# Moving small VectorE passes to GpSimd and ScalarE, and transposing all keys of the first batch by TensorE, in a fused agent-attention and mixture-of-experts kernel

## The chip, the cores and the metric

The kernel runs on one core of one Trainium2 chip. The metric is the time of one execution in device microseconds. A core has TensorE (PE in the profile, its weight loads PEld), VectorE (DVE), ScalarE (ACT), GpSimd (POOL) and SyncE (SP), which here only issues transfers. Each engine works through its own queue in order and waits at semaphores for the others.

## The reference

For each of B = 4 batches of N = 11456 tokens with C = 128 channels there are 49 agents. The agents attend to the keys, and the queries attend to the agents; the result is the input `x` of a mixture of 8 experts of width 1024, where each token goes to the one expert with the highest logit.

```python
def _attn_ref(q, k, v, agents):
    scale = 1.0 / np.sqrt(q.shape[-1])
    def sm(a, b):
        s = scale * (a @ b.transpose(0, 2, 1))
        s = s - s.max(-1, keepdims=True)
        e = np.exp(s)
        return e / (e.sum(-1, keepdims=True) + 1e-09)
    return sm(q, agents) @ (sm(agents, k) @ v)

# x: the attention's result, 45824 x 128
xn = x / (norm(x) + 1e-06); en = expert_emb / (norm(expert_emb) + 1e-06)
logits = xn @ en.T / tau
expert_idx = argmax(logits)
gate_w = exp(logits - max)[expert_idx] / (sum(exp(logits - max)) + 1e-09)
out[i] = gate_w[i] * (relu(x[i] @ w1[e]) @ w2[e])      # e = expert_idx[i]
```

## The kernel before

**Tiling.** A batch is cut into 12 units, eleven of 8 x 128 tokens and one of 2 x 96. A unit of keys, queries or values is loaded as one tile (`kt`, `qt`, `vt`; L114). The FFN goes by tiles of 4 x 128 tokens, 23 a batch, in 8 steps of 128 hidden columns each: 184 steps a batch, 736 in all.

**Precision.** The fp32 operands of the large products are split into two float16 parts, a high part and the remainder. A unit of keys or queries goes through `split`: ScalarE squares it for its size (L297), four small VectorE passes on one column (`half_scale`, L179 to L186) make a power of two `hsc` and its inverse `hiv`, ScalarE writes the scaled high part (L301), GpSimd multiplies and subtracts for the low part (L303, L304), and SP issues a DMA transpose (L309). Then TensorE has three float16 products for each 128 tokens (`scores`, L318 to L320). For queries, the inverse scale is multiplied with `escale` (L186), which holds the attention's scale. In a second way, `k1_f32`, TensorE transposes the fp32 unit itself (`pe_T`, L364), VectorE and ScalarE copy the result from PSUM, and TensorE scores it in fp32 (L382).

**Stages.** Nothing of the FFN can start until batch 0 has its agent values, since they are folded into the expert's weights. So there is a prelude: the 12 key units' scores (`k1`), the maximum over keys (`k_max`: a reduce, a transpose by TensorE, L151, L154, and the copy `pm`, L156), the 12 value units (`k2_unit`: `kd` = exp of the scores less the maximum, L400 and L402, and `avp`, `avx`, L408 to L414), then `av_chain` and `pick_expert`, which choose the batch's main expert, load its weights (`w1s`, `w2s`) and split them into `gh`, `gl`, `w2h`, `w2l`. Of batch 0's keys, units 1, 3, 5 and 7 (`K16`) go by `split` with `quick`, where VectorE makes the low part and ScalarE's own queue issues the DMA transpose; the other eight go by `k1_f32`. Between the value units stand other units, in a table `BETWEEN`: two queries of batch 0 and five key units of batch 1.

**Steady state.** In an FFN step TensorE makes `hp` (L722, L723), ScalarE `hh` = relu (L726), VectorE `hl`, the low part (L727), and four steps later (LAG) TensorE adds `yp` (L744 to L746) into one of two PSUM accumulators. After 8 steps `ffn_out` multiplies `yp` by the tokens' gates `gs` on VectorE (L759) and stores it. Beside the steps run the other queries (`queries`) and the keys and values of the next batch (`keys`), each a generator that issues a few instructions at a time. A query unit's softmax over agents (L572 to L576) gives `e`, which is split in two (L580 VectorE cast, L581 GpSimd), transposed (`tt`) and multiplied for the routing (`rtp`, `rtg`, `rt`, L598 to L617). For each group of one or two units `route_group` (L621) makes the gates `gs`: it takes norm, logits, their maximum and the softmax in small passes of 2 to 16 columns, or 8 times as many for the logits. There are 7 groups a batch. `mark_strays` and `stray` treat the tokens whose expert is not the main one.

**Order.** The order on each engine is set when the program is built: a scheduler with a simulated timeline places what the generators issue; in the prelude SP's order is that of the code.

## Time and profile before

| | |
|---|---|
| time, median of 3 executions | 1150.92 us (1150.88 to 1152.09) |
| time of the profiled execution | 1146.91 us, its span 1145.1 us |
| busy in the span: TensorE / VectorE / ScalarE / GpSimd | 1031.5 / 866.8 / 712.7 / 515.4 us |
| HBM traffic | 75.80 MB read, 23.53 MB written |

The table says how long each engine worked, not which one set the time; that is read stage by stage, from the rows in which an engine waits and what released it. In rows of the trace a start in us stands first, then the duration, the engine, the line, the operation and the tiles (out<-in), and in brackets the idle time ahead of it with what ended it. The profiled execution is 4.0 us shorter than the median of the others.

### The profile page before, as it was taken

The page shows a single profiled execution, that of the slowest core. Times are in us where ns is not written, and L with a number is a line of the kernel's source. Part 1 is how long each engine was busy: PE and PEld are TensorE (multiplying, and loading weights), DVE is VectorE, ACT ScalarE, POOL GpSimd, SP SyncE. Part 2 cuts the span into 40 slices and gives each one's busy share as a digit, 9 for nine tenths or more (in the row PEclk, how much of TensorE's full clock was granted, in tenths as well). Part 3 has the DMA queues.
Part 4 walks back from the last instruction along what each step waited for, and adds up shares of the span by engine and source line. Part 5 has one row for each costly group of instructions (what it writes and reads, how often), then busy time and mean ns, then how long its engine had stood idle before and what let it go on. Part 6 is the DMA issues. An engine that isn't in the chain of part 4 may idle for free.

```text
span 1145.1 us, 34081 instructions
## 1 busy us (share of the span) xinstructions
PE 1031.5 (90%) x13878; PEld 815.1 (71%) x13878; DVE 866.8 (76%) x2056; ACT 712.7 (62%) x1338; POOL 515.4 (45%) x449
## 2 busy tenths in 40 slices
PE   4677788999998888889999889999999799999997
PEld 4666566777777766667777667777778577887776
DVE  5446787877787778768688688877678889787785
ACT  4454967776657866756654876665455756655553
POOL 2262688756512986535430677354221624242100
PEclk9557899999999899999999899999999899999999
DMA  9959879953456997654433997733203534331100
GB/s 322 181 150 166 266 163 235 240 141 104 80 105 221 206 230 139 147 103 119 92 87 80 271 240 176 150 72 80 59 22 108 119 65 137 100 81 46 41 29 33
DMA packets 292264, 154.72 MB, mean 135 GB/s; under 512 B 216635, under 2 KB 268939, under 8 KB 292107
## 3 DMA queue, kind: packets, MB, share of 16 engines
q1 hardware_dynamic: 283723, 150.44, 54.9%
q10 hardware_dynamic: 8320, 2.10, 1.3%
q8 instruction: 109, 1.79, 0.6%
q14 instruction: 48, 0.39, 0.1%
q0 software_dynamic: 64, 0.00, 0.0%
HBM read 75.80 MB, written 23.53 MB: 87 GB/s over the span
## 4 chain that ended last, share of the span: by engine, by line
PE 53%; DMA 14%; issue 11%; DVE 9%; POOL 7%; ACT 4%; SPq 1%; ACTq 0%; POOLq 0%; DVEq 0%
PE hp L722 9%; PE yp L744 9%; PE yp L746 9%; PE yp L745 9%; PE hp L723 9%; PE avp L408 4%; DMA tt<-e 4%; DMA kt<-in_k_dram 3%; DVE hl L727 3%; DMA kT<-ks 2%; DMA qT<-qs 2%; POOL qt L303 2%; POOL kt L303 1%; POOL ks L304 1%; ACT hh L726 1%
## 5 line engine op out<-in xcount | busy, mean ns | idle before, releaser
L727 DVE SCALAR_TENSOR_TENSOR hl<-hp,hh 128x512 f16<-128x512 f32 (+1 forms) x736 | 479.6, 669 | 112.3 <-ACT hh L726 91.9
L726 ACT ACTIVATE hh<-hp 128x512 f16<-128x512 f32 (+1 forms) x736 | 416.5, 585 | 223.7 <-PE yp L745 132.4
L744 PE MATMUL yp<-w2h,hh 128*128 128x128 f16 (+1 forms) x2880 | 523.3, 220 | 6.4 <-ACT hh L726 6.2
L745 PE MATMUL yp<-w2l,hh 128*128 128x128 f16 (+1 forms) x2880 | 523.0, 220 | 2.7 <-DVE w2l L533 2.7
L746 PE MATMUL yp<-w2h,hl 128*128 128x128 f16 (+1 forms) x2880 | 522.4, 220 | 0.0
L744 PEld LDWEIGHTS <-hh 128*128 128x128 f16 (+1 forms) x2880 | 285.2, 99 | 61.5 <-ACT hh L726 8.5
L746 PEld LDWEIGHTS <-hl 128*128 128x128 f16 (+1 forms) x2880 | 285.6, 99 | 46.5 <-issue 3.9
L722 PE MATMUL hp<-tt,gh 128*128 128x512 f16 (+1 forms) x736 | 279.2, 379 | 40.0 <-DVE hl L727 35.3
L745 PEld LDWEIGHTS <-hh 128*128 128x128 f16 (+1 forms) x2880 | 285.2, 99 | 38.4 <-issue 0.3
L723 PE MATMUL hp<-tt,gl 128*128 128x512 f16 (+1 forms) x736 | 278.8, 379 | 0.0
L615 POOL TENSOR_TENSOR rt<-rt,qe 128x392 f32<-128x392 f32 (+1 forms) x48 | 46.3, 965 | 163.2 <-ACT rt L614 163.1
L303 POOL TENSOR_TENSOR qt<-qt,hsc 128x1024 f32<-128x1024 f32 (+1 forms) x46 | 81.9, 1783 | 66.2 <-ACT qs L301 52.8
L723 PEld LDWEIGHTS <-gl 128*128 128x128 f16 x736 | 72.5, 99 | 48.3 <-issue 46.3
L581 POOL TENSOR_TENSOR e<-qe,e 128x392 f16<-128x392 f32 (+1 forms) x48 | 41.5, 865 | 140.0 <-DVE e L580 62.9
L304 POOL TENSOR_TENSOR qs<-qt,qs 128x1024 f16<-128x1024 f32 (+1 forms) x46 | 93.1, 2027 | 0.6
L303 POOL TENSOR_TENSOR kt<-kt,hsc 128x1024 f32<-128x1024 f32 (+1 forms) x36 | 64.4, 1790 | 57.5 <-ACT ks L301 57.5
L722 PEld LDWEIGHTS <-gh 128*128 128x128 f16 x736 | 72.5, 98 | 10.0 <-issue 9.0
L304 POOL TENSOR_TENSOR ks<-kt,ks 128x1024 f16<-128x1024 f32 (+1 forms) x36 | 73.0, 2028 | 0.6
L759 DVE TENSOR_TENSOR ot<-yp,gs 128x512 f32<-128x512 f32 (+1 forms) x92 | 61.4, 668 | 14.5 <-PE yp L746 13.9
L646 POOL TENSOR_TENSOR nrm<-quad,half 128x16 f32<-128x16 f32 (+2 forms) x28 | 68.4, 2443 | 2.0
L408 PE MATMUL avp<-vt,kd 128*64 128x129 f32 x720 | 62.8, 298 | 5.1 <-ACT kd L402 4.8
L297 ACT ACTIVATE qs<-qt 128x1024 f16<-128x1024 f32 (+1 forms) x46 | 46.0, 1001 | 31.6 <-DMA qt<-in_q_dram 13.9
(258 smaller groups left out, 1483.7 us busy)
## 6 DMA issues: line engine op xcount, KB each, us to landing
kt<-in_k_dram SPq DMA_DIRECT2D x44, 512.0 KB, 6.0
qt<-in_q_dram SPq DMA_DIRECT2D x44, 512.0 KB, 7.0
vt<-in_v_dram SPq DMA_DIRECT2D x44, 512.0 KB, 5.4
out_dram<-ot SPq DMA_DIRECT2D x88, 256.0 KB, 2.2
w1s<-in_moe_w_dram SPq DMA_DIRECT2D x5, 512.0 KB, 3.6
w2s<-in_moe_w_dram SPq DMA_DIRECT2D x5, 512.0 KB, 4.9
qT<-qs SPq DMA_TRANSPOSE x46, 4.7
tt<-e SPq DMA_TRANSPOSE x46, 2.9
```

Of the source, the lines that this page charges most:

```text
L303: pool.tensor_tensor(out=s[:p, :n], in0=s[:p, :n], in1=sc.unsqueeze(2).broadcast_to([p, n, D]), op=ALU.mult)
L304: pool.tensor_tensor(out=xs[:p, :n, 1], in0=s[:p, :n], in1=xs[:p, :n, 0], op=ALU.subtract)
L408: pe.matmul(out=avp[hs, :W], lhsT=de[:p, c * A : c * A + LO], rhs=src[:p, c, :], start=(c < 2), stop=(c >= n - 2), skip_group_check=True)
L646: pool.tensor_tensor(out=nrm, in0=quad[:, :n], in1=half[:, :n], op=ALU.pow)
L722: pe.matmul(out=hp[:, :m], lhsT=bt.gh[:, fs], rhs=tt, start=True, stop=False)
L723: pe.matmul(out=hp[:, :m], lhsT=bt.gl[:, fs], rhs=tt, start=False, stop=True)
L726: act.activation(hh[:, :m], hp[:, :m], AF.Relu)
L727: dve.scalar_tensor_tensor(out=hl[:, :m], in0=hp[:, :m], scalar=0.0, in1=hh[:, :m], op0=ALU.max, op1=ALU.subtract)
L744: pe.matmul(out=y, lhsT=hh[:, cs], rhs=bt.w2h[:, f, :], start=(f == 0 and c == 0), stop=False, skip_group_check=True)
L745: pe.matmul(out=y, lhsT=hh[:, cs], rhs=bt.w2l[:, f, :], start=False, stop=False, skip_group_check=True)
L746: pe.matmul(out=y, lhsT=hl[:, cs], rhs=bt.w2h[:, f, :], start=False, stop=last, skip_group_check=True)
L759: dve.tensor_tensor(out=o[:p, :n], in0=yp[:p, :n], in1=gate, op=ALU.mult)
```

## The change

All of batch 0's keys now go by `k1_f32`; `K16` and `quick` are gone. `BETWEEN` keeps the two query units and has two key units of batch 1 in place of five; the other three go to `keys`. On VectorE, the multiplication by `escale` becomes part of the integer subtraction ahead of it (`qbias`, with the attention's scale now in the agents, `sga_s`), and products of two single columns become `tensor_scalar`. The cast of `e` goes to ScalarE; its low part stays on GpSimd, but goes to VectorE for the first two query units. For batches 1 to 3 `w2l` is made in two GpSimd passes in place of one on VectorE. In `route_group` VectorE keeps two reduces and two reciprocals; the maximum is now taken of the raw logits; GpSimd gets seven small passes, ScalarE the last product. One addition in `mark_strays` goes to GpSimd.

```diff
...
-    def half_scale(ssq, kexp, tag, bufs=2, fold=None):
+    def half_scale(ssq, kexp, tag, bufs=2, bias=float(254 * ONE)):
...
         yield 1
-        dve.tensor_scalar(iv.bitcast(I32), si, -1.0, float(254 * ONE), ALU.mult, ALU.add)
-        if fold is not None:
-            yield 1
-            dve.tensor_scalar(iv, iv, fold[:p], None, ALU.mult)
+        dve.tensor_scalar(iv.bitcast(I32), si, -1.0, bias if isinstance(bias, float) else bias[:p], ALU.mult, ALU.add)
         return sc, iv
...
     sga, isga = now_run(pow2(now_run(allmax(amx, 1, "amxr", pss, 0)), 10, "sga"))
+    sga_s = cst.tile([P, 1], F32, name="sga_s")
+    dve.tensor_scalar(sga_s, sga, SCALE, None, ALU.mult)
     escale = cst.tile([P, 1], F32, name="escale")
-    dve.tensor_scalar(escale, isga, SCALE, None, ALU.mult)
+    dve.tensor_copy(escale, isga)
+    qbias = cst.tile([P, 1], F32, name="qbias")
+    dve.tensor_scalar(qbias, isga.bitcast(I32), float(127 * ONE), None, ALU.add)
     a16 = cst.tile([P, B, 2 * A], F16, name="a16")
-    act.activation(a16[:, :, :A], aT_all, AF.Copy, scale=sga)
-    dve.scalar_tensor_tensor(out=a16[:, :, A:], in0=aT_all, scalar=sga, in1=a16[:, :, :A], op0=ALU.mult, op1=ALU.subtract)
+    act.activation(a16[:, :, :A], aT_all, AF.Copy, scale=sga_s)
+    dve.scalar_tensor_tensor(out=a16[:, :, A:], in0=aT_all, scalar=sga_s, in1=a16[:, :, :A], op0=ALU.mult, op1=ALU.subtract)
...
-    def split(kind, b, u, g, quick=False):
+    def split(kind, b, u, g):
...
         yield g
-        hs = half_scale(sq, 14, kind + "u", 4, escale if kind == "q" else None)
-        sc, iv = now_run(hs) if quick else (yield from hs)
+        hs = half_scale(sq, 14, kind + "u", 4, *([qbias] if kind == "q" else []))
+        sc, iv = yield from hs
         act.activation(xs[:p, :n, 0], s[:p, :n], AF.Copy, scale=sc)
-        if not quick:
-            pool.tensor_tensor(out=s[:p, :n], in0=s[:p, :n], in1=sc.unsqueeze(2).broadcast_to([p, n, D]), op=ALU.mult)
-            pool.tensor_tensor(out=xs[:p, :n, 1], in0=s[:p, :n], in1=xs[:p, :n, 0], op=ALU.subtract)
-        else:
-            dve.scalar_tensor_tensor(out=xs[:p, :n, 1], in0=s[:p, :n], scalar=sc, in1=xs[:p, :n, 0],
-                                     op0=ALU.mult, op1=ALU.subtract)
+        pool.tensor_tensor(out=s[:p, :n], in0=s[:p, :n], in1=sc.unsqueeze(2).broadcast_to([p, n, D]), op=ALU.mult)
+        pool.tensor_tensor(out=xs[:p, :n, 1], in0=s[:p, :n], in1=xs[:p, :n, 0], op=ALU.subtract)
         xT = wk.tile([P, 2 * UJ, P], F16, name=kind + "T", tag="xT", bufs=XB)
-        (act if quick else sp).dma_start_transpose(out=xT[:, : 2 * n, :p], in_=xs[:p, :n].rearrange("p c h d -> p (c h d)"))
+        sp.dma_start_transpose(out=xT[:, : 2 * n, :p], in_=xs[:p, :n].rearrange("p c h d -> p (c h d)"))
         return xT, iv
...
-    def k1_unit(b, u, g, quick=False):
+    def k1_unit(b, u, g):
         kb = blk_of(b, u)
...
             yield 1
-        xT, iv = yield from split("k", b, u, g[0], quick)
+        xT, iv = yield from split("k", b, u, g[0])
         yield g[1]
...
         spv = s[:p, : n * A].rearrange("p (c a) -> p c a", a=A)
-        act.activation(st, spv, AF.Copy, scale=sga[:p])
-        run_max(kb, spv, sga, p, n)
+        act.activation(st, spv, AF.Copy, scale=sga_s[:p])
+        run_max(kb, spv, sga_s, p, n)
         kb.s[u] = st
...
         sg2 = sm.tile([P, 1], F32, name="sg2", tag="sg2")
-        dve.tensor_tensor(out=sg2, in0=bt.sg, in1=bt.sg, op=ALU.mult)
+        dve.tensor_scalar(sg2, bt.sg, bt.sg, None, ALU.mult)
         r_hi = sm.tile([P, RW], F16, name="r_hi", tag="r_hi")
...
         sgw = sm.tile([P, 1], F32, name="sgw", tag="sgw")
-        dve.tensor_tensor(out=sgw, in0=s2, in1=bt.sg, op=ALU.mult)
+        dve.tensor_scalar(sgw, s2, bt.sg, None, ALU.mult)
         if b > 0:
...
         yield 1
-        dve.scalar_tensor_tensor(out=w2l, in0=w2s, scalar=s3, in1=w2h, op0=ALU.mult, op1=ALU.subtract)
+        if b == 0:
+            dve.scalar_tensor_tensor(out=w2l, in0=w2s, scalar=s3, in1=w2h, op0=ALU.mult, op1=ALU.subtract)
+        else:
+            pool.tensor_tensor(out=w2s, in0=w2s, in1=s3.unsqueeze(2).broadcast_to([P, NF, D]), op=ALU.mult)
+            pool.tensor_tensor(out=w2l, in0=w2s, in1=w2h, op=ALU.subtract)
         bt.w2h, bt.w2l = w2h, w2l
...
         iall = sm.tile([P, 1], F32, name="iall", tag="iall")
-        dve.tensor_tensor(out=iall, in0=bt.isg, in1=i2, op=ALU.mult)
-        yield 1
-        dve.tensor_tensor(out=iall, in0=iall, in1=i3, op=ALU.mult)
+        dve.tensor_scalar(iall, bt.isg, i2, None, ALU.mult)
+        yield 1
+        dve.tensor_scalar(iall, iall, i3, None, ALU.mult)
         bt.iall = iall
...
         hi = e2[:p, :n, :A]
-        dve.tensor_copy(hi, e)
-        pool.tensor_tensor(out=e2[:p, :n, LO : LO + A], in0=e, in1=hi, op=ALU.subtract)
+        act.copy(hi, e)
+        (dve if f32 else pool).tensor_tensor(out=e2[:p, :n, LO : LO + A], in0=e, in1=hi, op=ALU.subtract)
         tt = wk.tile([P, UJ * P], F16, name="tt", tag="tt", bufs=LEAD + 2)
...
+        rmx = small("rmx")
+        dve.tensor_reduce(out=rmx, in_=rtg[:, :n, :E], axis=AX.X, op=ALU.max)
         pool.tensor_scalar(quad[:, :n], quad[:, :n], 1e-36, None, ALU.max)
-        l = small("l")
-        dve.tensor_scalar(l.unsqueeze(2), rtg[:, :n, E:], 1e-9, None, ALU.add)
-        yield 1
         nrm = small("nrm")
         pool.tensor_tensor(out=nrm, in0=quad[:, :n], in1=half[:, :n], op=ALU.pow)
+        l, ls = small("l"), small("ls")
+        pool.tensor_scalar(l.unsqueeze(2), rtg[:, :n, E:], 1e-9, None, ALU.add)
+        pool.tensor_tensor(out=ls, in0=l, in1=bt.sg6.broadcast_to([P, n]), op=ALU.mult)
+        pool.tensor_tensor(out=nrm, in0=ls, in1=nrm, op=ALU.add)
         yield 2
-        dve.scalar_tensor_tensor(out=nrm, in0=l, scalar=bt.sg6, in1=nrm, op0=ALU.mult, op1=ALU.add)
-        yield 1
+        lg = bt.lg[:, cols]
+        pool.tensor_tensor(out=lg, in0=rtg[:, :n, :E], in1=bc(rmx, E), op=ALU.subtract)
         cc = small("cc")
...
         yield 1
-        lg = bt.lg[:, cols]
-        dve.tensor_tensor(out=lg, in0=rtg[:, :n, :E], in1=bc(cc, E), op=ALU.mult)
-        yield 1
-        lmx = small("lmx")
-        dve.tensor_reduce(out=lmx, in_=lg, axis=AX.X, op=ALU.max)
-        yield 1
-        dve.tensor_tensor(out=lg, in0=lg, in1=bc(lmx, E), op=ALU.subtract)
+        pool.tensor_tensor(out=lg, in0=lg, in1=bc(cc, E), op=ALU.mult)
         yield 1
...
         el = small("el")
-        dve.scalar_tensor_tensor(out=el, in0=es, scalar=1e-9, in1=l, op0=ALU.add, op1=ALU.mult)
+        pool.tensor_scalar(el, es, 1e-9, None, ALU.add)
+        pool.tensor_tensor(out=el, in0=el, in1=l, op=ALU.mult)
         yield 1
...
         yield 1
-        dve.tensor_scalar(gs[:, :n], gs[:, :n], bt.iall, None, ALU.mult)
+        act.activation(gs[:, :n], gs[:, :n], AF.Copy, scale=bt.iall)
         gss[b, gi] = gs
...
         dve.reciprocal(ga, ga)
-        dve.tensor_tensor(out=oh, in0=oh, in1=iota8m.unsqueeze(1).broadcast_to([P, NCOL, E]), op=ALU.add)
+        pool.tensor_tensor(out=oh, in0=oh, in1=iota8m.unsqueeze(1).broadcast_to([P, NCOL, E]), op=ALU.add)
         yield 1
...
-    K16 = (1, 3, 5, 7)
     QF = 2
-    BETWEEN = {2: ("k", 1, 0), 3: ("q", 0, 2), 4: ("k", 1, 1), 5: ("q", 0, 3), 6: ("k", 1, 2), 7: ("k", 1, 3), 8: ("k", 1, 4)}
+    BETWEEN = {1: ("q", 0, 2), 5: ("q", 0, 3), 8: ("k", 1, 0), 11: ("k", 1, 1)}
     NEXT = sum(x[0] == "k" for x in BETWEEN.values()) if B > 1 else 0
...
                 if b == 0:
-                    spawn(k1_unit(b, u, (1, 4), True) if u in K16 else k1_f32(b, u))
+                    spawn(k1_f32(b, u))
                 else:
```

The order shows what moves. The number behind a name tells tiles apart; line numbers of the changed kernel differ by up to 2 (its L362 and L380 are L364 and L382 of before, L299, L303, L304 and L305 are L297, L301, L303 and L304, L383 is L385, L727, L728 and L760 are L726, L727 and L759).

TensorE in the key scores of batch 0, before: `fTp` are transposes of a unit, `sp` its scores, `kT` the DMA-transposed float16 keys.

```order
L382 MATMUL sp_190<-aT_all_96,fT_168 128x49 x8
L364 MATMUL fTp_332<-ident_82,kt_161 128x128 x4
L382 MATMUL sp_233<-aT_all_96,fT_211 128x49 x8
L364 MATMUL fTp_338<-ident_82,kt_161 128x128 x4
L364 MATMUL fTp_408<-ident_82,kt_165 128x128 x4
L318 LDWEIGHTS kT_209
L318 MATMUL sp_282<-a16_128,kT_209 128x49
L319 LDWEIGHTS kT_209
```

The same engine and place after:

```order
L380 MATMUL sp_322<-aT_all_96,fT_272 128x49 x8
L362 MATMUL fTp_395<-ident_82,kt_169 128x128 x4
L362 MATMUL fTp_401<-ident_82,kt_169 128x128 x4
L380 MATMUL sp_352<-aT_all_96,fT_304 128x49 x8
L362 MATMUL fTp_423<-ident_82,kt_186 128x128 x4
L362 MATMUL fTp_429<-ident_82,kt_186 128x128 x4
L380 MATMUL sp_382<-aT_all_96,fT_334 128x49 x8
L362 MATMUL fTp_451<-ident_82,kt_202 128x128 x4
L362 MATMUL fTp_457<-ident_82,kt_202 128x128 x4
L362 MATMUL fTp_479<-ident_82,kt_230 128x96 x2
L380 MATMUL sp_410<-aT_all_96,fT_364 128x49 x8
```

The float16 products with the transposed keys are gone; each unit has eight fp32 transposes and eight fp32 products.

ScalarE around the maximum over keys (`pm`), before. `kt_698` and `kt_724` are key units of batch 1, `e16`/`tt` belong to the first query.

```order
L385 ACTIVATE s_u_553<-sp_544,p2s_120 128x392
L385 ACTIVATE s_u_575<-sp_572,p2s_120 96x98
L301 ACTIVATE ks_834<-kt_698,hsc_866 128x8x128
L576 ACTIVATE qe_589<-qe_589 128x392
L587 COPY tt_594<-tp_595 128x1024
L369 COPY fT_605<-fTp_606 128x512
L156 COPY pm_630<-mB_628 128x49
L297 ACTIVATE ks_890,usq_889<-kt_724 128x8x128
L402 ACTIVATE kd_0_144<-kd_0_144,escale_126 128x392
```

After, where `kt_645` is the first key unit of batch 1 and `qt_515` the fourth query unit, whose split also releases the buffer and the issue of `kt_645`'s load:

```order
L303 ACTIVATE qs_721<-qt_515,hsc_724 128x8x128
L383 ACTIVATE s_u_498<-sp_489,sga_s_126 128x392
L383 ACTIVATE s_u_520<-sp_517,sga_s_126 96x98
L578 ACTIVATE qe_534<-qe_534 128x392
L582 CAST e16_0_151<-qe_534 128x8x49
L299 ACTIVATE ks_804,usq_803<-kt_645 128x8x128
L589 COPY tt_539<-tp_540 128x1024
L303 ACTIVATE ks_804<-kt_645,hsc_808 128x8x128
L367 COPY fT_550<-fTp_551 128x512
L156 COPY pm_575<-mB_573 128x49
L400 ACTIVATE kd_0_148<-kd_0_148,escale_128 128x392
```

The first pass over a freshly loaded key unit of batch 1 (`kt_645`, L299) now stands ahead of `pm`; before, the only such pass there was the second one over a unit in hand (`kt_698`), and that of the next load stood behind `pm`.

GpSimd in the first FFN steps, before, with the gate of the second group (`nrm_1394`) and split passes (L303, L304):

```order
L641 TENSOR_SCALAR quad_1203<-quad_1203 128x16
L303 TENSOR_TENSOR kt_1252<-kt_1252,hsc_1533 128x1024
L304 TENSOR_TENSOR qs_1381<-qt_1256,qs_1381 128x8x128
L646 TENSOR_TENSOR nrm_1394<-quad_1203,half_132 128x16
L303 TENSOR_TENSOR kt_1254<-kt_1254,hsc_1746 128x1024
L304 TENSOR_TENSOR ks_1509<-kt_1252,ks_1509 128x8x128
L303 TENSOR_TENSOR qt_1258<-qt_1258,hsc_1890 128x1024
L615 TENSOR_TENSOR rt_1442<-rt_1442,qe_1052 128x392
```

After (`nrm_1180`, `lga_1046` belong to the second group; L304 and L305 are the split passes):

```order
L648 TENSOR_TENSOR nrm_1180<-quad_1005,half_136 128x16
L304 TENSOR_TENSOR kt_1064<-kt_1064,hsc_1454 128x1024
L305 TENSOR_TENSOR ks_1230<-kt_1062,ks_1230 128x8x128
L304 TENSOR_TENSOR kt_1224<-kt_1224,hsc_1611 128x1024
L617 TENSOR_TENSOR rt_1271<-rt_1271,qe_1038 128x392
L652 TENSOR_TENSOR nrm_1180<-ls_1183,nrm_1180 128x16
L304 TENSOR_TENSOR qt_1068<-qt_1068,hsc_1754 128x1024
L305 TENSOR_TENSOR ks_1433<-kt_1064,ks_1433 128x8x128
L304 TENSOR_TENSOR kt_1402<-kt_1402,hsc_1757 128x1024
L305 TENSOR_TENSOR ks_1558<-kt_1224,ks_1558 128x8x128
L583 TENSOR_TENSOR e16_0_151<-qe_1527,e16_0_151 128x8x49
L659 TENSOR_TENSOR lga_1046<-lga_1046,cc_1201 128x128
```

The group's passes now stand with split passes between them. VectorE where the second group's gates are first used, before (`gs_1470` is the first group's, `gs_1555` the second's, `hl` counts the steps):

```order
L671 RECIPROCAL gs_1555<-el_1531 128x16
L179 TENSOR_SCALAR hsc_2343<-usq_2321 128x1
L727 SCALAR_TENSOR_TENSOR hl_1851<-hp_1847,hh_1850 128x512
L675 TENSOR_SCALAR gs_1555<-gs_1555,iall_1182 128x16
L181 TENSOR_SCALAR hsc_2343<-hsc_2343 128x1
L727 SCALAR_TENSOR_TENSOR hl_1873<-hp_1869,hh_1872 128x512
L727 SCALAR_TENSOR_TENSOR hl_1903<-hp_1899,hh_1902 128x512
L759 TENSOR_TENSOR ot_1893<-yp_1660,gs_1470 128x512
```

After, where `gs_1306` is the second group's:

```order
L728 SCALAR_TENSOR_TENSOR hl_2359<-hp_2355,hh_2358 128x512
L672 RECIPROCAL gs_1306<-el_1281 128x16
L339 SCALAR_TENSOR_TENSOR m_run_763<-sp_2198,hiv_1910,m_run_763 128x392
L760 TENSOR_TENSOR ot_2020<-yp_1770,gs_1306 128x512
L760 TENSOR_TENSOR ot_2302<-yp_2033,gs_1306 128x512
L183 TENSOR_SCALAR hiv_2549<-hsc_2548 96x1
L728 SCALAR_TENSOR_TENSOR hl_2415<-hp_2411,hh_2414 128x512
```

The two output passes `ot` stood apart before, the first with the first group's gates; now the second group's reciprocal is followed by two output passes of that group in a row.

## The prediction

> **What bounds the kernel now.** I read the table of stages first, since shares over the whole span mix stages with different limits. Its columns are the stretch and its length, then busy time (and instructions) of TensorE, its weight loads, VectorE, ScalarE and GpSimd, the granted clock, the DMA share and GB/s.
>
> ```profile
> 0.00:67.00 67.00, 38.67 (x285) 35.19 (x285) 31.28 (x98) 30.25 (x51) 21.45 (x41) 0.70 0.93 231
> 67.00:79.00 12.00, 8.65 (x48) 8.30 (x48) 3.82 (x9) 3.24 (x6) 5.88 (x6) 0.56 0.81 190
> 79.00:106.00 27.00, 20.38 (x291) 17.25 (x290) 19.82 (x41) 13.66 (x23) 10.50 (x9) 0.81 0.93 159
> 106.00:124.00 18.00, 14.18 (x150) 10.97 (x151) 9.33 (x42) 11.05 (x25) 6.46 (x7) 0.62 0.97 285
> 124.00:232.00 108.00, 92.56 (x1281) 71.70 (x1280) 89.65 (x199) 82.29 (x153) 85.83 (x65) 0.95 0.92 209
> 232.00:1145.00 913.00, 857.05 (x11829) 671.69 (x11826) 712.93 (x1672) 572.22 (x1083) 385.33 (x324) 0.98 0.48 115
> ```
>
> The stretches are the key scores of batch 0, its maximum over keys, its value products, its agent values and expert weights, the first FFN steps with the rest of the key and query work beside them, and the rest. From 232 us on TensorE is busy 857 of 913 us: it bounds, and all that is to be had is 56 us of gaps and the little of slow clock. From 124 to 232 four engines are busy 82 to 93 of 108 us: nothing there is free. Before 124 us TensorE is busy 82 of 124 us at clocks of 0.56 to 0.81: a chain.
>
> Then the step rate, by counting the FFN's activation (one a step) in three stretches, and what ends TensorE's idle time from 124 us on (total, times, longest):
>
> ```profile
> 124.00:232.00 108.00, 40.14 (x71) 0.95 0.92 209
> 232.00:1145.00 913.00, 376.41 (x665) 0.98 0.48 115
> 700.00:1100.00 400.00, 178.46 (x309) 0.99 0.35 85
> PE hp L722 <- DVE hl L727: 35.3, 33, 4.1
> ```
>
> The steps take 1.52, 1.37 and 1.29 us. The last is the calm pace; 665 steps at it would take 861 us, 52 less than they do. The one large wait is for VectorE's `hl`. Why is VectorE late at times, when it is busy only 78% of that stretch? The groups of the passes that the change removes there (from 124 us on; busy us, mean ns) and one of the places show it:
>
> ```profile
> L580 DVE CAST e<-qe 128x392 f16<-128x392 f32 (+1 forms) x44 | 22.3, 506 | 1.9 <-ACT qe L576 1.6 <-issue 0.2
> L643 DVE TENSOR_SCALAR l<-rtg 128x16 f32<-128x16 f32 (+2 forms) x27 | 21.1, 783 | 1.6 <-ACT rtg L613 1.5
> L675 DVE TENSOR_SCALAR gs<-gs,iall 128x16 f32<-128x16 f32 (+2 forms) x28 | 16.2, 577 | 0.3
> L659 DVE TENSOR_TENSOR lga<-lga,lmx 128x128 f32<-128x128 f32 (+2 forms) x28 | 14.8, 529 | 0.2
> L668 DVE SCALAR_TENSOR_TENSOR el<-esa,l 128x16 f32<-128x16 f32 (+2 forms) x28 | 13.9, 498 | 0.5
> L654 DVE TENSOR_TENSOR lga<-rtg,cc 128x128 f32<-128x128 f32 (+2 forms) x27 | 12.5, 462 | 0.1
> L648 DVE SCALAR_TENSOR_TENSOR nrm<-l,sg,nrm 128x16 f32<-128x16 f32 (+2 forms) x27 | 11.0, 408 | 1.8 <-POOL nrm L646 1.6
> L186 DVE TENSOR_SCALAR hiv<-hiv,escale 128x1 f32<-128x1 f32 (+1 forms) x44 | 9.0, 205 | 0.3
> L533 DVE SCALAR_TENSOR_TENSOR w2l<-w2s,hsc,w2h 128x1024 f16<-128x1024 f32 x4 | 6.8, 1706 | 0.1
> ```
> ```profile
> L643 DVE TENSOR_SCALAR l<-rtg x28: 154/174/4958, 116.7 to 1088.2; 128x16 f32<-128x16 f32 x20, 128x8 f32<-128x8 f32 x4, 128x2 f32<-128x2 f32 x4
> 403.13 4.96 DVE L643 TENSOR_SCALAR l<-rtg 128x16 f32<-128x16 f32 x1
> 403.11 2.12 POOL L304 TENSOR_TENSOR qs<-qt,qs 128x1024 f16<-128x1024 f32 x1
> 405.20 1.89 POOL L303 TENSOR_TENSOR qt<-qt,hsc 128x1024 f32<-128x1024 f32 x1
> 407.05 1.00 POOL L615 TENSOR_TENSOR rt<-rt,qe 128x392 f32<-128x392 f32 x1
> 409.21 0.58 PE L722 MATMUL hp<-tt,gh 128*128 128x512 f16 x1 [4.11 <-DVE hl L727]
> 409.20:412.10 2.90, 2.89 (x21) 1.98 (x21) 2.34 (x7) 1.82 (x5) 0.91 (x1) 0.50 0.38 104
> 412.10:416.00 3.90, 3.90 (x57) 3.30 (x56) 2.45 (x7) 3.90 (x7) 1.30 (x1) 0.99 1.05 230
> ```
>
> The small pass L643 has a median of 174 ns and a longest of 4958 ns. That longest one starts 0.02 us after a GpSimd pass and ends 0.04 us after the third of an unbroken run of them. So a 128x16 VectorE pass with SBUF operands stands still while GpSimd works; behind it `hl` is late, TensorE idles 4.11 us, and then runs 2.9 us at clock 0.50. A removed pass thus takes away its own time and such a stall.
>
> **The change part by part. Main stage.** From VectorE leave the nine groups above, the last with 3 of its 4: 22.3+21.1+16.2+14.8+13.9+12.5+11.0+9.0+5.1 = 126 of the 803 us that it is busy from 124 us on. L657's reduce stays as `rmx`. What TensorE gets of it is only what ends a wait: the 35.3 us above. By place, 31 us of TensorE's gaps in that stretch follow a stretched pass of a removed kind, about 25 of them after 232 us. Five of these stalls are followed by slow clock of 2.9 to 6.8 us, at half speed, 1.5 to 3.4 us each, some 9 us. That is 34 us after 232. I keep 28: the casts and gate factors put new work ahead of ScalarE's `hh`, and the second gates of batches 1 and 2 come late in the order, as those of batch 0 below. Least: 12 us, if other small passes with SBUF operands catch the same GpSimd runs and the removed ones only passed the stall on; most: the 52 us to the calm pace.
>
> The costs there. GpSimd gets seven small passes for each of 28 groups, `w2l` three times, and one addition for each batch's strays; ScalarE gets the casts and the gate's last factor:
>
> ```profile
> L641 POOL TENSOR_SCALAR quad<-quad 128x16 f32<-128x16 f32 x20 | 5.5, 273 | 13.8 <-DVE quad L617 13.7
> L615 POOL TENSOR_TENSOR rt<-rt,qe 128x392 f32<-128x392 f32 x44 | 44.8, 1018 | 146.9 <-ACT rt L614 146.8
> L304 POOL TENSOR_TENSOR ks<-kt,ks 128x1024 f16<-128x1024 f32 x33 | 71.0, 2153 | 0.6
> 116.58 0.49 ACT L614 COPY rt<-rtp 128x392 f32<-128x392 f32 x1
> ```
>
> A gate group: five at 0.27 and two 128x128 at about 0.45 (between 0.27 for 16 columns and 1.02 for 392) = 2.3, so 63 us; `w2l` 3 x 4.1 = 12; the addition 4 x 1.7 = 7. That makes 385+60 of 913 us after 232: still half idle. Its waits are in order, though, and the chain of a gate now crosses GpSimd, VectorE and ScalarE. In the order most gates stand one to three output passes ahead of their use, so I cost this at nothing but for the places named; the cover is that slack. ScalarE: 44 x 0.49 + 28 x 0.25 = 29 us, beside 572 of 913: hidden, as long as nothing that it waits for is late. The fold of the scale into the integer bias, `tensor_scalar` for `tensor_tensor` on single columns, and the scale's place in the agents cost nothing: the count of instructions there is the same or less.
>
> **First FFN steps (124 to 232).** Three of the five key units of batch 1 that were split in the prelude come here. Each is 4.05 us of GpSimd (2.15+1.90), 2.8 of ScalarE, 1.1 of VectorE: GpSimd gets 12 us for them and 7 for three gate groups on top of 86 of 108, which makes 105. By the order, split passes stand among the second group's gate passes, and its first two tiles are written out together after step 38, where they were written at 29 and 36. A tile not written out holds one of the two accumulators, so TensorE stops at step 36 until the gate is there. GpSimd has some 20 split passes (20 x 2.0 = 40), the routing's products and the gate passes to do until then, about 55 us if it never waits, and 36 steps at 1.52 us take 55: the stop is 0 if all goes well, and some steps if GpSimd waits. Against it stand 6 us of stalls that go here. I take +3, with -8 (only the stalls go) and +15 (12 us of splits and 3 of stops on the path) as bounds.
>
> **Prelude.** K16's four units were split as later ones are, with a DMA transpose issued by ScalarE; now all twelve are transposed and scored by TensorE in fp32.
>
> ```profile
> 18.10 8.40 ACTq L309 DMA_TRANSPOSE kT<-ks  x1
> 35.28 9.90 ACTq L309 DMA_TRANSPOSE kT<-ks  x1
> PE sp L318 <- DMA kT<-ks: 7.2, 1, 7.2
> 7.67 1.97 PE L364 MATMUL fTp<-ident,kt 128*128 128x128 f32 x8
> 14.09 1.99 PE L382 MATMUL sp<-aT_all,fT 128*128 128x49 f32 x16
> 7.00:19.60 12.60, 11.51 (x73) 10.19 (x73) 7.98 (x31) 8.37 (x15) 0.33 (x3) 1.00 1.03 398
> 62.08 4.29 PE L382 MATMUL sp<-aT_all,fT 128*128 128x49 f32 x20 [1.79 <-DVE m_run L341]
> 67.07 3.65 PE L564 MATMUL sp<-aT_all,fT 128*128 128x49 f32 x16 [0.70 <-DVE m_run L341]
> 74.00 1.03 PE L586 MATMUL tp<-ident,e 128*128 128x128 f16 x8 [3.28 <-POOL vt L109]
> ```
>
> ScalarE's own queue stood 8.4 and 9.9 us in the issue of a transpose, and TensorE waited 7.2 us for one. Without them a unit costs TensorE 1.97 + 1.99 = 3.96 us at full clock (ScalarE needs 1.2 and VectorE 1.3 for it, so TensorE sets the pace). 11.25 units from 7.67 us and the first query's 3.96 end at 56.2; the last scores come without transposes between them, as at 62.08, where a unit takes 3.4 instead of 2, so 2.5 more: 58.7 against 70.7 now. From there to the maximum the stall of 3.28 us goes (the query's low part goes from GpSimd to VectorE). But a new wait comes: ScalarE and VectorE have the first pass of a key unit of batch 1 ahead of the copy and the reduce of the maximum, and that key's load stands on SP behind the GpSimd split of the fourth query (ScalarE 1.2, GpSimd 4.05, the load about 6, ScalarE 1.1, VectorE 0.5), which begins at about 50. So the maximum comes at 66, not at 79. The value products lose about 3 of these 13, since ScalarE stands at the next key's load there as well, and the expert's weights, on SP now behind four transposes, another 3. The term is -7; between -20 (none of the losses, and the clock full) and +11 (K phase at half clock: 18 us later).
>
> **Sum**: -7 + 3 - 28 = -32 us. The profiled execution is 1146.9 us, 4.0 us under the median of the runs, 1150.9; of the execution -32 makes 1115, of the median 1119. I forecast 1119. The execution's span is 1.8 us below its own time, which nothing here changes.
>
> **The rivals.**
> 1. *All of it.* The prelude gains 14 and the main stage runs at the calm pace throughout, 52: 1151-66 = 1085. For it: 309 steps in 400 us already do. Against: loads and k units fill the first half of each batch.
> 2. *The clock stays at half in the K phase.* TensorE then pays 18 us more there: 1137. Against it: from 7.0 to 19.6 us, where two units' scores take 3.9 of the 11.5 busy us and nearly all the rest is transposes, the clock was 1.00. For it: the scores alone from 62 us on never got it back. The Trainium skill, "TensorE: Matmul & The Clock Gate", Part 4 on the PE-mode transpose, says that transposes do not count as work for the clock gate; by that rule the K phase, half of it transposes, would stay slow, and the time would be this rival's. The row from 7.00 on speaks against the rule.
> 3. *GpSimd gives the waits back.* The gate passes on GpSimd queue behind 2 us splits, and what VectorE no longer waits for, it waits for as a consumer: only the prelude's 7 us remain, 1144. For it: the three passes 403.11 to 408.05 in a row. Against: the slack of 26 us and more. The Trainium skill, "Perfetto Trace Analysis", Optimizing Scalar/DVE Operations, warns that the two engines share a read port, so that moving work between them might not help; by it the main stage would gain nothing. The rows above agree that they get in each other's way, but GpSimd's 2.12 us beside a standing VectorE is its mean of 2.15, so the loser is VectorE alone, and it is the loser that gets less to do.
> 4. *Slower: ScalarE stands at the gate's last factor.* That product is in ScalarE's queue ahead of `hh`, behind VectorE's reciprocal, behind GpSimd's last gate passes. If one split pass of 2.15 us is ahead of these at each of the 28 groups, `hh` is late by it, and TensorE with it: 60 us, 1119+60 = 1179. It decides from 32/28 = 1.1 us a group. Against: the later gates come long before use, and in the order the reciprocal is some steps ahead of the product.
>
> **How the numbers follow.** My forecast 0.55 (its own range 1104 to 1134), rival 1 0.10, rival 2 0.10, rival 3 0.13, rival 4 0.12. The range takes the forecast, rival 2, most of rival 3 and the near half of rival 1: 1090 to 1147. 0.2%, 2.3 us, is what a measurement of this kernel can tell from no change. Rival 4 is slower (0.12), rival 3 is the same in a third of its cases (0.04), the rest is faster: 0.84.
>
> **What the profile after would show.** Right: TensorE's wait for `hl` from the FFN's start on falls from 35 us to under 10, no VectorE pass of a 128x16 tile lasts over 1 us, the steps after the first 70 take under 1.33 us, the last key scores end near 55 us at clock near 1, and the FFN starts at about 117. Wrong: `hh` waits for `gs` on ScalarE, TensorE's wait for `hh` over 15 us, the `yp` matmuls wait for the output pass near steps 32 to 40, or a clock of 0.5 from 20 to 55 us.

## The result, and the profile after

| | before | after |
|---|---|---|
| time, median | 1150.90 us (1147.72 to 1152.09, 4 runs) | 1108.26 us (1104.85 to 1112.14, 4 runs) |
| profiled execution, its span | 1146.91, 1145.1 us | 1104.85, 1103.1 us |
| VectorE, GpSimd, ScalarE busy | 866.8, 515.4, 712.7 us | 770.4, 581.2, 724.9 us |

The ratio is 0.9635, 95% interval 0.9597 to 0.9673: 43 us less, where 32 were forecast. The table of stages after, with stretches cut at the same events as before (last key scores, maximum over keys, last value products, first FFN step, 70th step):

```profile
0.00:47.00 47.00, 37.82 (x287) 36.59 (x287) 29.62 (x78) 19.50 (x34) 14.05 (x39) 0.92 0.85 273
47.00:57.00 10.00, 6.85 (x35) 6.20 (x34) 3.95 (x10) 4.67 (x8) 1.24 (x3) 0.51 0.18 52
57.00:84.00 27.00, 18.24 (x228) 16.34 (x228) 17.80 (x32) 12.21 (x21) 9.21 (x7) 0.81 0.46 107
84.00:103.00 19.00, 13.29 (x127) 9.78 (x126) 8.90 (x41) 10.40 (x24) 6.44 (x10) 0.59 1.00 288
103.00:205.00 102.00, 90.28 (x1313) 68.94 (x1312) 70.49 (x167) 85.24 (x160) 90.07 (x78) 0.98 0.98 213
205.00:1103.00 898.00, 854.21 (x11894) 671.26 (x11892) 639.63 (x1455) 592.92 (x1162) 460.18 (x520) 0.99 0.51 122
```

The first stretch is 20 us shorter; the three behind it are 10, 27 and 19 us where they were 12, 27 and 18. So nearly all of the prelude's gain, 21 us, lies in the key scores. From the first FFN step to the end it was 1145.1 - 124.3 = 1020.8 us, and is 1103.1 - 103.1 = 1000.0: another 21 us. By the last two rows of each table TensorE is idle there for 71 us before and 56 after, and busy for 950 and 944, at clocks of 0.95 and 0.98 before and 0.98 and 0.99 after. ScalarE's first `hh` stands at these two times, in before and in after:

```profile
124.26 0.62 ACT L726 ACTIVATE hh<-hp 128x512 f16<-128x512 f32 x1
```
```profile
103.08 1.12 ACT L727 ACTIVATE hh<-hp 128x512 f16<-128x512 f32 x2
```

TensorE's waits from the first FFN step on, before (the wait for `hl` was 35.3 us) and after:

```profile
PE rtp L598 <- DMA tt<-e: 9.8, 10, 3.2
PE yp L744 <- ACT hh L726: 6.2, 5, 2.2
```
```profile
PE hp L723 <- DVE hl L728: 15.6, 27, 1.9
PE rtp L600 <- DMA tt<-e: 14.8, 13, 2.9
PE yp L745 <- ACT hh L727: 9.2, 9, 2.8
...
PE yp L745 <- DVE ot L760: 0.8, 2, 0.5
```

The wait for `hl` lost 20 us and its longest is 1.9 in place of 4.1 us. Eight of the 20 came back as longer waits for the transposed `tt` and for `hh`. The wait for the output pass, on which the gates of the second group could have acted, is 0.8 us.

Then the key scores, in which a unit's eight transposes and sixteen rows of scores alternate:

```profile
21.35 1.05 PE L362 MATMUL fTp<-ident,kt 128*128 128x128 f32 x8
22.25 1.88 PE L380 MATMUL sp<-aT_all,fT 128*128 128x49 f32 x16
23.97 1.05 PE L362 MATMUL fTp<-ident,kt 128*128 128x128 f32 x8
24.86 1.88 PE L380 MATMUL sp<-aT_all,fT 128*128 128x49 f32 x16
...
38.93 7.03 PE L380 MATMUL sp<-aT_all,fT 128*128 128x49 f32 x36 [1.54 <-DVE m_run L339]
```

A unit comes every 2.62 us (23.97 - 21.35), not 3.96, until the tail of scores alone at 38.93: 7.03 us for 36 rows, 0.195 us each where 16 rows took 1.88, 0.118 each. The tail ran at half the clock:

```profile
39.70:47.00 7.30, 6.60 (x33) 6.44 (x32) 2.77 (x8) 2.55 (x4) 3.27 (x2) 0.50 0.32 85
```

### The profile page after: what moved, and what is told of

Read it like the earlier page. It is cut to its first block, busy times and chain, and to the rows that moved or that the text cites. A ratio compares the mean times of both kernels' runs of the same rounds, so it can differ in the third digit from the quotient of the medians.

```text
span 1103.1 us, 33928 instructions
## 1 busy us (share of the span) xinstructions
PE 1020.7 (93%) x13878; PEld 809.1 (73%) x13878; DVE 770.4 (70%) x1779; ACT 724.9 (66%) x1406; POOL 581.2 (53%) x653
## 4 chain that ended last, share of the span: by engine, by line
PE 55%; DMA 13%; POOL 11%; issue 8%; ACT 5%; DVE 5%; SPq 1%; POOLq 0%; ACTq 0%; DVEq 0%
PE hp L723 9%; PE yp L745 9%; PE hp L724 8%; PE yp L746 8%; PE yp L747 8%; DMA tt<-e 5%; PE avp L406 4%; DMA kT<-ks 3%; DMA qt<-in_q_dram 3%; POOL qs L305 2%; POOL ks L305 2%; POOL kt L304 2%; PE sp L380 2%; POOL qt L304 2%; ACT hh L727 1%
## 5 line engine op out<-in xcount | busy, mean ns | idle before, releaser
L728 DVE SCALAR_TENSOR_TENSOR hl<-hp,hh 128x512 f16<-128x512 f32 (+1 forms) x736 | 480.8, 670 | 140.4 <-ACT hh L727 114.5
L727 ACT ACTIVATE hh<-hp 128x512 f16<-128x512 f32 (+1 forms) x736 | 415.8, 588 | 181.9 <-PE yp L746 136.2
L745 PEld LDWEIGHTS <-hh 128*128 128x128 f16 (+1 forms) x2880 | 284.3, 99 | 63.5 <-ACT hh L727 12.4
L723 PE MATMUL hp<-tt,gh 128*128 128x512 f16 (+1 forms) x736 | 276.6, 376 | 19.8 <-DVE hl L728 15.6
L304 POOL TENSOR_TENSOR qt<-qt,hsc 128x1024 f32<-128x1024 f32 (+1 forms) x46 | 82.0, 1784 | 49.1 <-ACT qs L303 42.1
L305 POOL TENSOR_TENSOR qs<-qt,qs 128x1024 f16<-128x1024 f32 (+1 forms) x46 | 92.2, 2007 | 0.5
L304 POOL TENSOR_TENSOR kt<-kt,hsc 128x1024 f32<-128x1024 f32 (+1 forms) x36 | 64.5, 1791 | 41.9 <-ACT ks L303 41.6
L650 POOL TENSOR_SCALAR l<-rtg 128x16 f32<-128x16 f32 (+2 forms) x28 | 8.2, 292 | 128.5 <-ACT rtg L615 127.7
L583 POOL TENSOR_TENSOR e<-qe,e 128x392 f16<-128x392 f32 (+1 forms) x46 | 39.7, 864 | 68.6 <-ACT e L582 57.6
L305 POOL TENSOR_TENSOR ks<-kt,ks 128x1024 f16<-128x1024 f32 (+1 forms) x36 | 72.9, 2025 | 0.6
L760 DVE TENSOR_TENSOR ot<-yp,gs 128x512 f32<-128x512 f32 (+1 forms) x92 | 61.4, 670 | 8.9 <-PE yp L747 8.2
L299 ACT ACTIVATE qs<-qt 128x1024 f16<-128x1024 f32 (+1 forms) x46 | 46.3, 1006 | 31.9 <-DMA qT<-qs 10.6
```

The source lines that it names most:

```text
L304: pool.tensor_tensor(out=s[:p, :n], in0=s[:p, :n], in1=sc.unsqueeze(2).broadcast_to([p, n, D]), op=ALU.mult)
L305: pool.tensor_tensor(out=xs[:p, :n, 1], in0=s[:p, :n], in1=xs[:p, :n, 0], op=ALU.subtract)
L723: pe.matmul(out=hp[:, :m], lhsT=bt.gh[:, fs], rhs=tt, start=True, stop=False)
L727: act.activation(hh[:, :m], hp[:, :m], AF.Relu)
L728: dve.scalar_tensor_tensor(out=hl[:, :m], in0=hp[:, :m], scalar=0.0, in1=hh[:, :m], op0=ALU.max, op1=ALU.subtract)
L745: pe.matmul(out=y, lhsT=hh[:, cs], rhs=bt.w2h[:, f, :], start=(f == 0 and c == 0), stop=False, skip_group_check=True)
```

## The experiments

All ratios are to the kernel before on the same chip, with 95% intervals; its median was 1145.0 to 1145.4 us in these measurements. The table gives when some FFN steps began, by the start of their `hh` in the profiled executions. The first two rows are the kernels compared.

| run | ratio | first step | step 72 | step 184 | end of span |
|---|---|---|---|---|---|
| before | 1 | 124.3 | 234.1 | 396.3 | 1145.1 |
| after | 0.9635 [0.9597, 0.9673] | 103.1 | 212.5 | 373.5 | 1103.1 |
| e1, prelude only | 0.9954 [0.9934, 0.9975] | 102.0 | 219.6 | 389.3 | 1137.7 |
| e2, passes only | 0.9767 [0.9744, 0.9789] | 123.7 | 228.2 | 388.8 | 1117.0 |
| e7, no next keys in the prelude | 0.9555 [0.9519, 0.9591] | 93.3 | 204.7 | 368.0 | 1094.8 |
| e10, five next keys | 0.9612 [0.9576, 0.9648] | 102.3 | 207.6 | 366.0 | 1097.1 |
| e9, before with transposes from SP | 0.9918 [0.9886, 0.9951] | 112.2 | 222.7 | 385.9 | 1134.6 |

**The prelude alone (e1).** The kernel before with

```diff
-    K16 = (1, 3, 5, 7)
-    BETWEEN = {2: ("k", 1, 0), 3: ("q", 0, 2), 4: ("k", 1, 1), ...}
+    K16 = ()
+    BETWEEN = {1: ("q", 0, 2), 5: ("q", 0, 3), 8: ("k", 1, 0), 11: ("k", 1, 1)}
```

> The kernel before, with only the prelude of the change: all keys of batch 0 by fp32 transposes, and the new table of units between the values. Theory (the two halves of the change add up): the FFN starts at 103 to 106 us as after, and from there on the steps take as long as before (1021 us in the trace, hl waits some 35 us): 1130 us, range 1125 to 1135. Rival (the three key units that come later crowd the first FFN steps and give the gain back): FFN start 103 to 106, but step 72 is reached no more than 10 us earlier than before, 1140 to 1151.

It gained 0.46%, 5.3 us. The FFN began 22 us earlier, but step 72 was only 14.5 and step 184 only 7 us earlier. From step 0 to 90 it took 152 us; before took 135. Its waits in that stretch, and the stretch's row:

```profile
PE hp L722 <- DVE hl L727: 8.6, 7, 3.4
PE rtp L598 <- DMA tt<-e: 6.9, 3, 2.7
PE yp L745 <- DVE w2l L533: 4.3, 1, 4.3
```
```profile
102.00:254.00 152.00, 127.03 (x1749) 97.71 (x1749) 118.50 (x257) 110.62 (x202) 114.46 (x86) 0.92 0.86 201
```

The three longest are 20 us of its 25 us without TensorE, and the clock is 0.92 in place of 0.96 before. So the rival came near here: by itself the shorter prelude gives two thirds of its gain back, though later than the rival had it, since 14.5 us and not 10 were left at step 72. That the three later key units are the cause is not shown: one of the three waits is for `w2l`, and in e7 below, with all twelve of them beside the FFN but the passes moved, the same 90 steps take 137 us.

**The passes alone (e2).** The changed kernel with K16's path and table of before (`K16`, `quick`, the old `BETWEEN` put back).

> The changed kernel with the prelude of before: units 1, 3, 5 and 7 of batch 0's keys by DMA transposes from ScalarE's queue, and the old table of units between the values. Theory (the halves add up): the FFN starts at 121 to 126 us, and from there to the end 1000 us, as after; TensorE's wait for hl under 20 us: 1130 us, range 1125 to 1135. Rival (the moved passes gain nothing by themselves, what was gained behind the prelude comes from the new order there): 1143 to 1151.

2.3%, 27 us: more than the theory's 20. The first FFN step is where it was before, and the rest takes 993 us, 28 less than before.

```profile
PE hp L727 <- DVE hl L732: 14.4, 27, 2.2
PE yp L749 <- ACT hh L731: 13.3, 12, 3.0
PE rtp L604 <- DMA tt<-e: 7.9, 9, 1.8
```

The wait for `hl` is that of after. The two parts alone multiply to 0.9954 x 0.9767 = 0.972; together they give 0.9635. They do not simply add: with the passes moved, the first 90 steps after the earlier start take 134 us and not 152, so the prelude's gain mostly stays.

**Unused VectorE passes put in**, six for each gate group, in the old forms (e3) or as reduces (e4):

```diff
+        dve.tensor_scalar(small("dm").unsqueeze(2), rtg[:, :n, E:], 1e-9, None, ALU.add)          # e3, and five more
+        dve.tensor_reduce(out=small("dm"), in_=rtg[:, :n, :E], axis=AX.X, op=ALU.max)             # e4, six times
```

> The changed kernel with six more VectorE passes in each gate group, in the forms and sizes that stood there before (128x16 and 128x128, operands in SBUF), whose results nobody uses. Theory (small passes with SBUF operands stand still beside GpSimd): they take 60 to 90 us in all, the longest over 2 us, TensorE's wait for hl goes back from 16 to 25 or 30 us, and the time goes up by 6 to 14 us, to 1114 to 1122. Rival (VectorE's load alone counts): the same time as the kernel with six reduces, within 3 us.

> The changed kernel with six more VectorE reduces (128x128 to 128x16) at the same six places of each gate group, whose results nobody uses. A reduce took 0.25 us each time in both traces. Theory (standing still is what costs): 28 x 6 x 0.25 = 42 us more of VectorE, none over 0.4 us, the wait for hl stays under 20 us, and the time is within 3 us of the changed kernel's 1108. Rival (load counts): up by as much as with the six passes of the old forms, 6 us or more.

The first gave 0.9721 [0.9696, 0.9745], the second 0.9750 [0.9726, 0.9774]: both slower than the changed kernel (0.9635) by about 1%, the second not less. Of the six groups in each, the one at the gate's end, with TensorE's waits, in e3 and then in e4:

```profile
L681 DVE TENSOR_SCALAR dm<-rmx,sg 128x16 f32<-128x16 f32 (+2 forms) x28 | 13.7, 490 | 0.0
```
```profile
PE hp L729 <- DVE hl L734: 17.9, 23, 4.0
```
```profile
L681 DVE TENSOR_REDUCE dm<-rtg 128x16 f32<-128x128 f32 (+2 forms) x28 | 6.9, 248 | 0.0
```
```profile
PE rtp L600 <- DMA tt<-e: 19.7, 12, 4.6
PE hp L729 <- DVE hl L734: 17.0, 22, 3.2
```

The old forms stood still as expected (490 ns each in this group, 70 us for the six), the reduces did not (248 ns, 41 us). But 41 us that never stood cost as much as 70 that did, and in both the wait for `hl` rose by no more than 2.3 us (from 15.6). My theory that standing still is what costs is not borne out here. That any load costs is what e4 fits, but by load alone e3, with 29 us more of it, would have been the slower one. A third cause can't be excluded: with six passes more, the scheduler placed everything anew. Of the 48 query units' `rtp`, 6 in e3 and 12 in e4 stand more than one FFN step from where they stood on TensorE. With one reduce of 8 values for each batch (e8), 46 of 48 stand where they stood, and the other two one step away:

> The changed kernel with one unused reduce of 8 values on VectorE in the first gate group of each batch: 4 passes of some 0.1 us, which leave the order of all engines as it was in nearly all places. It shows what the same kernel gives beside the others of this call. All theories: within 3 us of the changed kernel, a ratio to before of 0.960 to 0.967.

It took 0.9647 [0.9613, 0.9681], the changed kernel's time, and stands for it beside the next three. Its wait for `hl` is 13.7 us and that for `tt` 16.5, where the changed kernel has 15.6 and 14.8: differences of 2 us in these waits say nothing.

**One part of the moved passes back on VectorE**: the gate groups' (e5, `route_group` as before), or the cast of `e` (e6):

```diff
-        act.copy(hi, e)
+        dve.tensor_copy(hi, e)
```

> The changed kernel with the gate groups' passes on VectorE again, as before (and none of them on GpSimd or ScalarE). Theory (these passes stand still beside GpSimd and make hl late): they take 80 to 95 us again, the longest over 3 us, TensorE's wait for hl goes from 16 back to 25 to 33 us, and the time to 1118 to 1128. Rival (any 40 us of VectorE costs the same, as with the unused passes): wait for hl under 20 us, time 1117 to 1120. Second rival (the route's way over three engines costs as much as it gains): within 3 us of 1108.

> The changed kernel with the cast of e on VectorE again. Theory (VectorE's passes beside GpSimd stall TensorE): 20 us more of VectorE, some casts over 1 us, time up by 3 to 7 us to 1111 to 1115. Rival (the casts delay ScalarE's hh as much as they free VectorE): within 2 us, with TensorE's wait for hh down from 9 to 6 us.

The gate passes back cost 1.1% (0.9759 [0.9726, 0.9793]), the cast 0.8% (0.9725 [0.9693, 0.9758]), against the 0.9647 above. Both are more than the rivals without a loss allowed (3 and 2 us). In e5 the passes stood still again (87 us for the six groups), and the wait for `hl` went up, if less than the theory's 25 to 33; the time, 1119, fits the theory and the rival of load alike:

```profile
L677 DVE TENSOR_SCALAR gs<-gs,iall 128x16 f32<-128x16 f32 (+2 forms) x28 | 21.2, 759 | 0.4
```
```profile
PE hp L724 <- DVE hl L729: 23.5, 37, 3.6
```

In e6 it rose less; the waits for `tt` grew as in e4. In the profiled execution 10 us were lost by step 72 (222.8 against 212.5), and up to there the wait for `tt` is 6.3 us in place of 0.7:

```profile
PE rtp L600 <- DMA tt<-e: 20.1, 15, 4.9
PE hp L723 <- DVE hl L728: 19.2, 27, 3.7
```

So taking back either one costs: the gate passes in part through `hl`, the cast through the queries' way to `tt` and `rtp`. But here too the scheduler placed much anew: 13 and 16 of the 48 units' `rtp` stand more than one step away, more than in e4. What of the 1.1 and 0.8% is the passes' own, and what comes of the order, is not separated.

**Key units of batch 1 in the prelude**: none (e7), or the old five (e10), in place of two.

```diff
-    BETWEEN = {1: ("q", 0, 2), 5: ("q", 0, 3), 8: ("k", 1, 0), 11: ("k", 1, 1)}
+    BETWEEN = {1: ("q", 0, 2), 5: ("q", 0, 3)}
```

> The changed kernel with no key unit of batch 1 in the prelude (all 12 come beside the FFN). Theory (a key unit split beside the first FFN steps costs them more than its place in the prelude): the FFN starts at 97 to 101 us, 2 to 6 us earlier, but step 90 is reached 2 to 8 us later after that start, and the time is 1108 to 1114. Rival (the later units are hidden, the gain of the prelude stays): 1102 to 1106.

> The changed kernel with the old table of units between the values: five key units of batch 1 in the prelude in place of two. Theory (each split on GpSimd there makes VectorE's kd passes stand and costs the prelude some 5 us, more than it costs beside the FFN): FFN start at 110 to 120 us, time 1114 to 1122. Rival (order of the first FFN steps decides, units that are done early save as much there): FFN start 110 to 120, time within 4 us of 1108.

None is the fastest kernel of the study: 0.9555 [0.9519, 0.9591], 1095.4 us where e8, measured beside it, took 1105.5. That is less than theory and rival had. Its FFN begins at 93.3, 10 us earlier, and 8 of these stay. Five (e10) are not told from two, and their interval overlaps with that of none; its FFN start, 102.3, and its time, 1099.5, lie outside what theory and rival had. VectorE's `kd` passes between maximum and value products show where most of the 10 us were. In after, all twelve of them (shortest, median, longest in ns), then two places in the timeline, with GpSimd's passes there:

```profile
L398 DVE TENSOR_TENSOR kd<-s_u,pm x12: 244/556/2484, 57.2 to 79.3; 128x392 f32<-128x392 f32 x11, 96x98 f32<-96x98 f32 x1
```
```profile
57.17 4.65 DVE L398 TENSOR_TENSOR kd<-s_u,pm 128x392 f32<-128x392 f32 x3
...
76.62 2.29 DVE L398 TENSOR_TENSOR kd<-s_u,pm 128x392 f32<-128x392 f32 x1
```
```profile
56.62 1.89 POOL L304 TENSOR_TENSOR kt<-kt,hsc 128x1024 f32<-128x1024 f32 x1
58.59 2.33 POOL L305 TENSOR_TENSOR ks<-kt,ks 128x1024 f16<-128x1024 f32 x1
...
76.15 2.33 POOL L305 TENSOR_TENSOR ks<-kt,ks 128x1024 f16<-128x1024 f32 x1
```

The same without the key units:

```profile
L398 DVE TENSOR_TENSOR kd<-s_u,pm x12: 247/556/570, 58.7 to 72.1; 128x392 f32<-128x392 f32 x11, 96x98 f32<-96x98 f32 x1
```
```profile
58.69 1.52 DVE L398 TENSOR_TENSOR kd<-s_u,pm 128x392 f32<-128x392 f32 x3 [1.75 <-ACT pm L156]
```

Without a GpSimd pass beside them none takes over 570 ns, and the twelve keep VectorE busy for 6.2 us in place of 12.7. The last one begins at 72.1 in place of 79.3, though the maximum came 1.5 us later; the agent values' chain behind them is shorter by 2.6 us. Three passes that take 1.52 us alone took 4.65 beside a split. So here, where one chain sets the end, the 6.5 us of standing still are most of the gain. They are not separated from the rest of the two key units: ScalarE, for one, waited 1.8 us at 70.3 for the second one's load.

That five units cost no more than two fits the same account. In e10 the passes take

```profile
L398 DVE TENSOR_TENSOR kd<-s_u,pm x12: 246/556/2284, 56.0 to 76.7; 128x392 f32<-128x392 f32 x11, 96x98 f32<-96x98 f32 x1
```

and of its five splits on GpSimd three end by 57.0 us, when the passes have just begun. Two stand beside them, from 63.4 and 71.5 us, as many as in the changed kernel. The theory's price of some 5 us for each split can at most hold for those beside the passes.

**The keys spread wider (e11, e12)**, on top of none in the prelude: batch 1's keys over 40 or 50% of the first batch's steps.

```diff
-        W_ = [(0, 0.25, 0.3, 0.8), ...]
+        W_ = [(0, 0.4, 0.42, 0.82), ...]      # and (0, 0.5, 0.52, 0.86)
```

> The changed kernel with no key unit of batch 1 in the prelude, and its 12 key units spread over the first 40% of batch 0's steps in place of 25%. Theory (GpSimd, busy 98 of the first 107 us, holds up the first 70 steps): GpSimd under 90% there, step 72 reached in 104 to 108 us after the FFN's start in place of 111, time 1090 or less (ratio 0.946 to 0.952). Rival (the first steps are held by loads and by the route's chain, not by the amount on GpSimd): within 0.3% of the kernel without key units in the prelude, 0.9555.

> As the one before, with the keys of batch 1 over the first 50% of the steps, and its values from 52 to 86%. Theory: a little better in the first 70 steps, but the expert of batch 1 is ready later; the start of batch 1's steps (184) waits 0 to 8 us: ratio 0.945 to 0.956. Rival: as above, 0.9555 within 0.3%.

0.9627 [0.9593, 0.9660] and 0.9619 [0.9586, 0.9653]: no better than 0.9555 [0.9519, 0.9591], e11 just beyond its interval and e12 overlapping it, and neither theory nor rival had that. The first 72 steps did get shorter (109 and 107 us against 111), with GpSimd still busy for 101 of e11's 109 us, where the theory had it under 90%. But the gain was lost by step 184: it began 278 and 280 us after the FFN's start against 275. In part it was only moved: TensorE has 34 and 118 matmuls more there, between steps 72 and 184, than in e7. A late expert of batch 1 shows up to there as no more than one wait of 1.2 us for `gh` in e12. By the end both are 7 us behind e7; why is open.

**What made the key scores long (e9).** The kernel before, with

```diff
-        (act if quick else sp).dma_start_transpose(...)
+        sp.dma_start_transpose(...)
```

> The kernel before, with the DMA transposes of its four float16 key units issued by SP and not by ScalarE. Theory (ScalarE's queue standing 8.4 and 9.9 us in the issue is what made the key scores long): the last key score moves from 66 to 50-56 us and the FFN starts 8 to 14 us earlier. Rival (the transpose's own way, and TensorE's wait for it, is what counts, whoever issues it; SP then stands in it, and the loads behind it): the last key score at 62 us or later.

```profile
13.57 4.19 SPq L309 DMA_TRANSPOSE kT<-ks  x1
...
30.56 4.98 SPq L309 DMA_TRANSPOSE kT<-ks  x1
```
```profile
51.85 0.80 ACT L385 ACTIVATE s_u<-sp,p2s 128x392 f32<-128x392 f32 x2
```

The first and the last of SP's four issues, and then ScalarE's copy of the last scores: SP stands 3 to 5 us in the four, but ScalarE goes on; the last scores are copied at 51.9, where this row began at 65.8 before and at 45.4 after. So some 14 of the 20 us were ScalarE's queue. The other 6 came with the fp32 way, and the clock may be the reason: in e9 it was at half speed from 15.4 us on, though TensorE was busy, and in after it was full from 12.4 to 39.7.

```profile
0.00:52.00 52.00, 42.92 (x285) 41.18 (x285) 29.32 (x91) 27.83 (x46) 14.11 (x37) 0.65 0.99 287
```

The whole kernel gained 0.8%, about 9 of the 12 us by which its FFN began earlier.

## Why the prediction was right, and where it was off

The time, the sign and the range held, the time in part by luck: the prelude gained three times what I had put down for it, and the main stage two thirds. Of the sum -7 + 3 - 28 in the trace, -21.2, about -2 and -19 were measured (the 70th and the 72nd step give -3.2 and -0.5 for the second).

- *Prelude, -7 forecast, -21 measured.* The way was right, the size not. The step that failed is the price of a unit: I took 1.97 us for eight transposes from the first row, at 7.67, where later ones took 1.05, and added rows' lengths where the starts follow each other faster. I also took that row to be at full clock, and that is not shown: the traces have no record of the clock before 12.8 us (12.4 after), and the views count time without a record as 1.00. The unit's 2.62 us in place of 3.96, less a slow tail of 7 us, made the first query's scores end at 50.3, 8 us earlier than forecast (58.7). The stall of 3.28 us between them and the maximum, which I took as gone, is still there with 3.04. The two losses of 3 us (the value products, the expert's weights) did not come as a change from before: both stages were as long as they had been.
- *The wait of the maximum for a key's load.* Forecast at 66, 7 us behind the first query's scores, it came at 57, again 7 us behind them. That this agrees is luck. ScalarE's first pass over the key unit waited for nothing, and the transposes of the maximum stood in TensorE's queue behind the query's `tp`, which waited for the low part of `e`, now on VectorE:

```profile
52.59 1.05 ACT L299 ACTIVATE ks<-kt 128x1024 f16<-128x1024 f32 x1
53.35 1.03 PE L588 MATMUL tp<-ident,e 128*128 128x128 f16 x8 [3.04 <-DVE e L583]
```

  In e7 no key unit stood there, and `pm` came no earlier (58.5).
- *First steps, +3 forecast, about -2.* The gates of the second group came in time: TensorE waited 0.8 us for output passes.
- *Rest, -28 forecast, -19 measured.* The wait for `hl` fell by 20 of 35 us over the whole FFN, to 15.6 where I had said under 10. What I missed besides is that the waits for `tt` and `hh` grow by 8. VectorE's busy time from the first FFN step on fell by 92 us (803 to 710), not by the 126 that I had added up. The 666 steps from 205 us on take 1.35 us each, where I had said under 1.33. That no pass of a 128x16 tile lasts over 1 us any more came true.
- *The reason given for it*, that a removed pass takes a stall of another engine's making with it, is seen in the prelude (`kd`) and in before's trace, but not confirmed for the gate passes: e3 and e4 cost alike. What share of the passes' 27 us is VectorE's load, standing still, or the order, is open, and so it stays open why this term came to 19 and not 28.
- *Rival 2* fell but for its end: with transposes and scores in turn the clock was full for 27 us, as this row of a finer table of stages shows; only the tail of scores alone, and what follows up to 56.8 us, ran at half.

```profile
12.40:39.70 27.30, 25.76 (x234) 25.37 (x232) 18.50 (x49) 14.49 (x27) 4.98 (x11) 1.00 1.00 303
```

  The rule of the Trainium skill that it rested on ("TensorE: Matmul & The Clock Gate", Part 4 on the PE-mode transpose) is not borne out for these fp32 transposes: from 7.4 to 12.4 us TensorE had nothing else to do, and the clock's first record, from 12.4 on, is full.
- *Rival 3* fell with e2, where the passes alone gained 2.3%; so did the warning of "Perfetto Trace Analysis" in the Trainium skill for this case. *Rival 4* is there in small: ScalarE stood 9.4 us in all at the gate's last factor, 1.5 at the longest. TensorE's wait for `hh` rose by 3.0, but that fits the casts rather: it is 6.2 again with the cast back on VectorE (e6), and 8.1 with the gate passes back (e5).

```profile
ACT gs L676 <- DVE gs L672: 9.4, 9, 1.5
```

- *Rival 1* came half true: its prelude, not its main stage.
